# Staging buffers, cast placement and running ahead in the ramp of a fused RWKV-6 and GELU-MLP kernel

## The chip, the cores and the metric

The kernel runs on one core of one Trainium2 chip. The metric is the device time in microseconds (us), and it is taken over several executions. The kernel before takes 254.79 us (median of 3 runs, 253.57 to 255.71). A trace shows one of the executions.

The engines are named as in the profile: PE is the matmul engine (PEld is its weight load), DVE the vector engine, ACT the scalar engine, POOL the general engine, SP the engine whose queue issues the DMAs. "PEclk" or "granted clock" is the share of full speed that PE's clock was granted.

## The reference

A linear-attention recurrence over 768 steps for 4 sequences and 8 heads of width 48 gives a 3072 x 384 matrix. A two-layer MLP with a tanh-GELU follows.

```python
# r, k, v, w: (4, 8, 768, 48) float32; u: (8, 48)
for t in range(S):
    cur = np.einsum('bhd,bhe->bhde', u[None] * kt, vt)
    y[:, :, t] = np.einsum('bhd,bhde->bhe', rt, state + cur)
    state = wt[:, :, :, None] * state + np.einsum('bhd,bhe->bhde', kt, vt)
x = y.transpose(0, 2, 1, 3).reshape(B * S, H * D)        # 3072 x 384
h = x @ w_in                                            # 384 x 2048
g = 0.5 * h * (1.0 + np.tanh(c * (h + 0.044715 * h**3)))
out = g @ w_out                                         # 2048 x 384
```

## The kernel before

The work is cut into 12 units: 3 windows of 256 steps, times 4 sequences. They are numbered from 0. Each unit has these steps.

- `ln`: the log of the decay on ACT. `a1`: cumulative sums of it as matmuls ("cum" in the trace). `exps`: five exponentials on ACT.
- `prep`: on DVE k and r times decay (`kk`, `rq`) and a reduction `dg`; on POOL the cast of v (`vb`), two products for the diagonal (`rk`), the diagonal times v (`vsc`) and the decay masks `am`.
- `attention`, a generator of seven pieces: transposes of rq and kk on PE and their copies on DVE (tiles `T` and `TT`, a2), score matmuls and masks (`mt`, a3, twice), outputs and state (`y`, `p`, a4), two carry-over pieces with ACT copies (`xs`, a5), and the transpose of the result with a DVE copy (`xT`, a6).
- `mm1`: eight pieces of six matmuls each (`h`), each followed by a GELU on ACT (`g`). `mm2`: 32 matmuls (`o`) into two outputs, then `store`.

The kernel loads one function table on ACT for GELU and another for exp and ln, two in each unit. The 25 loads in the trace take 1283 ns each on average, and around one of them ACT goes from the end of a GELU to the start of an exponential in 1.31 us (100.19 to 101.50 us). In a steady unit q, mm1 and mm2 of unit q are threaded with the attention of unit q+1 and the preparation of unit q+2.

Weights arrive as float32 in staging tiles and are cast to bf16:

```python
pload = ctx.enter_context(tc.tile_pool(name="pload", bufs=5))
pstage = ctx.enter_context(tc.tile_pool(name="pstage", bufs=4))
# ...
def load_w_in(i):
    cb, hf = i % NCB, i // NCB
    t = pstage.tile([P, DF // 2], FP, tag="st", name=f"wi{i}")
    SP.dma_start(out=t, in_=moe_w_in[ts(cb, P), ts(hf, DF // 2)])
    stages["i", i] = t
def cast_w_in(i):
    cb, hf = i % NCB, i // NCB
    DVE.tensor_copy(out=w_in_sb[:, cb, ts(hf, DF // 2)], in_=stages.pop(("i", i)))
# load_w_out and cast_w_out alike: tag "st", cast on DVE
```

The start and the loop:

```python
table("exp"); ln(0); a1(0); exps(0)              # joined onto one line here
for i in range(6):
    load_w_in(i)
for nm in ("k", "r", "v"):
    load(1, nm)
ln(1)
prep(0)
load(2, "w")
for _ in attention(0):
    pass
for i in range(6):
    cast_w_in(i)
a1(1); exps(1); ln(2); prep(1)                   # joined here
for i in range(8):
    load_w_out(i)
for nm in ("k", "r", "v"):
    load(2, nm)
load(3, "w")
for q in range(NU):
    # ... loads of unit q+3 and w of unit q+4
    att = attention(q + 1) if q + 1 < NU else iter(())
    table("gelu")
    for i in range(8):
        mm1(q, i)
        if q == 0 and i >= 2:
            cast_w_out(i - 2)
        if i >= 2:
            mm2(q, 0, (2 * i - 4, 2 * i - 3))
        next(att, None)
        if i == 6 and q + 2 < NU:
            a1(q + 2)
    # q == 0: cast_w_out(6), cast_w_out(7)
    table("exp")
    # exps(q + 2), ln(q + 3)
    mm2(q, 0, range(12, 16))
    store(q, 0)
    # prep(q + 2)
    mm2(q, 1, range(16))
    store(q, 1)
    for _ in att:
        pass
```

Four staging tiles serve 14 loads, each load waits for a cast, and every cast stands in DVE's instruction order behind whatever comes before it there.

Of the kernel before, what the change touches and what calls it, by code (L numbers as in the profile page):

```python
# [9 lines left out]
FP = mybir.dt.float32  # L10
BF = mybir.dt.bfloat16
AF = mybir.ActivationFunctionType
AL = mybir.AluOpType
# [6 lines left out]
def kernel(  # L20
# [12 lines left out]
    PE, ACT, DVE, POOL, SP = nc.tensor, nc.scalar, nc.vector, nc.gpsimd, nc.sync  # L33

    B, H, S, D = r.shape
    P = 128
# [8 lines left out]
    NU = len(units)  # L45

    pconst = ctx.enter_context(tc.tile_pool(name="pconst", bufs=1))
    pload = ctx.enter_context(tc.tile_pool(name="pload", bufs=5))
    pstage = ctx.enter_context(tc.tile_pool(name="pstage", bufs=4))
    pfix = ctx.enter_context(tc.tile_pool(name="pfix", bufs=1))  # L50
    pw2 = ctx.enter_context(tc.tile_pool(name="pw2", bufs=2))
    pw3 = ctx.enter_context(tc.tile_pool(name="pw3", bufs=3))
# [10 lines left out]
    def load(q, nm):  # L63
        wi, b = units[q]
        src = {"r": r, "k": k, "v": v, "w": w}[nm]
        t = pload.tile([P, H, 2 * D], FP, tag=nm, name=f"{nm}{q}")
        ap = bass.AP(tensor=src.tensor, offset=src[b, 0, wi * WIN, 0].offset,
                     ap=[[2 * D, P], [S * D, H], [1, 2 * D]])
        SP.dma_start(out=t, in_=ap)
        ld[nm, q] = t  # L70
# [4 lines left out]

    def load_w_in(i):
        cb, hf = i % NCB, i // NCB
        t = pstage.tile([P, DF // 2], FP, tag="st", name=f"wi{i}")
        SP.dma_start(out=t, in_=moe_w_in[ts(cb, P), ts(hf, DF // 2)])
        stages["i", i] = t  # L80

    def cast_w_in(i):
        cb, hf = i % NCB, i // NCB
        DVE.tensor_copy(out=w_in_sb[:, cb, ts(hf, DF // 2)], in_=stages.pop(("i", i)))

    def load_w_out(i):
        t = pstage.tile([P, 2, HD], FP, tag="st", name=f"wo{i}")
        SP.dma_start(out=t, in_=moe_w_out[ds(i * 2 * P, 2 * P), :].rearrange(
            "(ft p) c -> p ft c", p=P))
        stages["o", i] = t  # L90

    def cast_w_out(i):
        DVE.tensor_copy(out=w_out_sb[:, ds(2 * i, 2), :], in_=stages.pop(("o", i)))  # L93

    for nm in ("w", "k", "r", "v"):
        load(0, nm)
# [51 lines left out]
    def table(which):  # L148
        if which == "exp":
            ACT.preload_act_table_set(EXP_SET)  # L150
        else:
            ACT.preload_act_table(AF.Gelu_apprx_tanh)  # L152

    def ln(q):
        lw = logws[q % 3]
        ACT.activation(  # L156
            out=lw[:, :, :, 0:D].rearrange("p t h d -> p h t d"),
            in_=ld.pop(("w", q)).rearrange("p h (t d) -> p h t d", t=2), func=AF.Ln)
# [26 lines left out]
    def prep(q):  # L185
        fq, e1, al = st.pop(("dec", q))
        kt, rt, vt = ld.pop(("k", q)), ld.pop(("r", q)), ld.pop(("v", q))
        kk, rq = kk_ps[q % 2], rq_ps[q % 2]

        def tdh(ap):  # L190
            return ap.rearrange("p h (t d) -> p t h d", t=2)

        def dec(ap):
            return ap.rearrange("p t (h d) -> p t h d", h=H)

        DVE.tensor_tensor(out=kk[:, :, :, 0:D], in0=tdh(kt), in1=dec(e1), op=AL.mult)
        DVE.tensor_tensor(out=rq[:, :, :, 0:D], in0=tdh(rt), in1=dec(fq), op=AL.mult)  # L197
        vb = pw2.tile([P, 2, H, D], BF, tag="vb", name=f"vb{q}")
        POOL.tensor_copy(out=vb, in_=tdh(vt))  # L199
        rk = pw2.tile([P, H, 2, D], FP, tag="rk", name=f"rk{q}", bufs=1)  # L200
        dg = pw2.tile([P, H, 2], FP, tag="dg", name=f"dg{q}")
        vsc = pw2.tile([P, 2, H, D], BF, tag="vsc", name=f"vsc{q}")
        am = pw2.tile([P, 2, G, 2 * D], FP, tag="am", name=f"am{q}")
        POOL.tensor_tensor(out=rk, in0=kt.rearrange("p h (t d) -> p h t d", t=2),  # L204
                           in1=rt.rearrange("p h (t d) -> p h t d", t=2), op=AL.mult)
        POOL.tensor_tensor(out=rk, in0=rk,  # L206
                           in1=u_bc[:, :, None, :].broadcast_to([P, H, 2, D]), op=AL.mult)
        DVE.tensor_reduce(out=dg, in_=rk, axis=AX.X, op=AL.add)  # L208
        POOL.tensor_tensor(  # L209
            out=vsc, in0=vb,  # L210
            in1=dg.rearrange("p h t -> p t h")[:, :, :, None].broadcast_to([P, 2, H, D]),
            op=AL.mult)
        for c2 in range(2):
            POOL.tensor_tensor(
                out=am[:, c2], in0=blk.rearrange("p g j d -> p g (j d)"),
                in1=al[:, :, c2][:, :, None].broadcast_to([P, G, 2 * D]), op=AL.mult)
        st["pre", q] = (kk, rq, vb, vsc, am)

    def a2(q, which):
        kk, rq, vb, vsc, am = st["pre", q]  # L220
# [117 lines left out]
    def mm2(q, c2, fts):  # L338
        g = st["g", q]
        for ft in fts:  # L340
            if ft == 0:
                st["o", q, c2] = ps_o.tile([P, HD], FP, tag="o", name=f"o{q}_{c2}")
            PE.matmul(st["o", q, c2], g[:, ft, ts(c2, P)], w_out_sb[:, ft, :],  # L343
                      start=(ft == 0), stop=(ft == NFT - 1))
# [15 lines left out]
    def attention(q):  # L360
        a2(q, 1)
        a2(q, 0)
        yield
        a3(q, 0)
        yield
        a3(q, 1)
        yield
        a4(q)
        a4p(q)
        yield  # L370
        a5(q, 0)
        yield
        a5(q, 1)
        yield
        a6(q)
        yield

    table("exp")
    ln(0)
    a1(0)  # L380
    exps(0)
    for i in range(6):
        load_w_in(i)
    for nm in ("k", "r", "v"):
        load(1, nm)
    ln(1)
    prep(0)
    load(2, "w")
    for _ in attention(0):
        pass  # L390
    for i in range(6):
        cast_w_in(i)
    a1(1)
    exps(1)
    ln(2)
    prep(1)
    for i in range(8):
        load_w_out(i)
    for nm in ("k", "r", "v"):
        load(2, nm)  # L400
    load(3, "w")
    for q in range(NU):
        if q + 3 < NU:
            for nm in ("k", "r", "v"):
                load(q + 3, nm)
        if q + 4 < NU:
            load(q + 4, "w")
        att = attention(q + 1) if q + 1 < NU else iter(())
        table("gelu")
        for i in range(8):  # L410
            mm1(q, i)
            if q == 0 and i >= 2:
                cast_w_out(i - 2)
            if i >= 2:
                mm2(q, 0, (2 * i - 4, 2 * i - 3))
            next(att, None)
            if i == 6 and q + 2 < NU:
                a1(q + 2)
        if q == 0:
            cast_w_out(6)  # L420
            cast_w_out(7)
        table("exp")
        if q + 2 < NU:
            exps(q + 2)
        if q + 3 < NU:
            ln(q + 3)
        mm2(q, 0, range(12, 16))
        store(q, 0)
        if q + 2 < NU:
            prep(q + 2)  # L430
        mm2(q, 1, range(16))
        store(q, 1)
        for _ in att:
            pass


# [28 lines left out]
```

## Time and profile before

| | before |
|---|---|
| median of 3 runs | 254.79 us |
| span of the profiled run | 253.7 us |
| unit 1's first mm1 on PE | 62.14 us |
| unit 2's first and third mm1 on PE | 86.32 and 90.30 us |
| distance between table loads, steady units | 17.06 us |

The page of the kernel before shows the span in 40 equal slices, each digit being a busy share in tenths. One slice is 6.3 us.

```profile
span 253.7 us, 5753 instructions
...
PE   1527333889289989899899898998998989989993
...
PEclk9999998589959999999999999999999999999999
DMA  8940893339984183291391742913916210020202
```

Read by columns, the first 12 slices (up to 76 us) form a ramp with holes in PE's row. After it PE is at 8 or 9. The DMA row falls to 0 in slice 4 and to 3 in slices 7 to 9, so loads stop in the middle of a phase that still waits for data. The clock falls to 5 in slices 8 and 12. The 9s of the clock row before that don't prove a full clock: this trace's first clock record is at 38.88 us, and the first mm1 piece of unit 0, at 25.77 us, took 1.52 us, where the same six matmuls take 0.82 us later.

The timeline of the DMA queue tells why the loads stop. The columns are start, duration, engine, line, operation and tiles.

```profile
8.79 0.43 SPq L79 DMA_DIRECT2D wi_188<-in_moe_w_in_dram  x1
25.02 0.33 SPq L79 DMA_DIRECT2D wi_190<-in_moe_w_in_dram  x1
...
35.25 0.42 SPq L88 DMA_DIRECT2D wo_411<-in_moe_w_out_dram  x1
45.16 0.37 SPq L88 DMA_DIRECT2D wo_413<-in_moe_w_out_dram  x1
48.37 0.37 SPq L88 DMA_DIRECT2D wo_415<-in_moe_w_out_dram  x1
53.71 0.37 SPq L88 DMA_DIRECT2D wo_417<-in_moe_w_out_dram  x1
...
55.77 3.32 SPq L69 DMA_DIRECT2D v_425<-in_v_dram  x1
```

After four tiles of w_in the queue stands from 9.2 to 25.02 us, until the first cast has freed a tile. It stands again three times between 35.7 and 53.7 us, and v of unit 2 (`v_425`) is behind it.

The waits of PE from 0 to 90 us give the price. The columns are the waiting tile and line, the releaser, the total, the number and the longest.

```profile
PE T_1_447 L225 <- DVE rq_128 L197: 8.3, 1, 8.3
PE mt_0_0_783 L238 <- DVE TT_0_773 L227: 5.7, 1, 5.7
...
PE mt_0_0_1081 L238 <- DVE TT_0_1071 L227: 0.8, 1, 0.8
```

The 8.3 us are unit 1's transposes, which wait for rq and so for unit 1's late r. The 5.7 us are unit 2's scores, which wait for copies that stand in DVE's order behind the reduction `dg`; that waits for POOL's products, which stand behind the cast of unit 2's v on POOL. The 0.8 us return in each steady unit.

PE's timeline shows what follows such a hole; an mm1 piece is six matmuls.

```profile
62.14 0.82 PE L334 MATMUL h_0_745<-xT_651,w_in_sb 128*128 128x256 bf16 x6
...
71.24 1.46 PE L334 MATMUL h_2_804<-xT_651,w_in_sb 128*128 128x256 bf16 x6
...
86.32 0.82 PE L334 MATMUL h_0_1043<-xT_952,w_in_sb 128*128 128x256 bf16 x6
```

A piece takes 0.82 us, but 1.46 us after the 5.7 us hole. The stretch view gives PE's busy time in one steady unit (columns: stretch, its length, then the busy time of each engine, the granted clock, the DMA share, GB/s).

```profile
100.20:117.26 17.06, 15.93 (x209) 11.30 (x208) 11.07 (x16) 10.58 (x19) 7.42 (x6) 1.00 0.52 117
```

So 1.1 us of each steady unit are PE waits.

### The profile page before, as it was taken

The numbers are of one execution on the slowest core, as the hardware profiler recorded it, in microseconds if no ns is written. First come the engines' busy times: TensorE is split into PE (matmuls) and PEld (weight loads), VectorE is DVE, ScalarE is ACT, GpSimd is POOL, SyncE is SP. The second block draws the span as 40 slices with busy tenths as digits, with TensorE's granted clock in tenths as the row PEclk, the third lists the DMA queues.
The fourth block names the chain that finished last, engine by engine and source line by source line (L and its number), as shares of the span: only waits on it lengthen the run. The fifth ranks groups of instructions, "written<-read, shape, count | busy, mean of one in ns | idle before, by whom it ended". The sixth has DMA issues, their size and how long they took to land.

```text
span 253.7 us, 5753 instructions
## 1 busy us (share of the span) xinstructions
PE 204.3 (81%) x2448; PEld 142.2 (56%) x2448; DVE 136.4 (54%) x220; ACT 128.8 (51%) x217; POOL 91.7 (36%) x84
## 2 busy tenths in 40 slices
PE   1527333889289989899899898998998989989993
PEld 0314132455148667576576675766766757657671
DVE  7566335356253663773855757738447377284101
ACT  3401213145514936756649368466584594654760
POOL 2570038000890091470740913806509228040000
PEclk9999998589959999999999999999999999999999
DMA  8940893339984183291391742913916210020202
GB/s 184 317 170 3 249 286 127 106 129 267 267 208 83 32 190 94 62 248 32 95 193 31 181 102 51 242 37 85 215 31 161 60 44 21 6 58 3 48 16 62
DMA packets 56969, 30.45 MB, mean 120 GB/s; under 512 B 50928, under 2 KB 56176, under 8 KB 56944
## 3 DMA queue, kind: packets, MB, share of 16 engines
q1 hardware_dynamic: 56944, 30.09, 48.3%
q8 instruction: 19, 0.31, 0.5%
q14 instruction: 6, 0.05, 0.1%
HBM read 25.36 MB, written 4.72 MB: 119 GB/s over the span
## 4 chain that ended last, share of the span: by engine, by line
PE 46%; DVE 17%; issue 15%; ACT 9%; POOL 7%; DMA 3%; SPq 1%; POOLq 0%; DVEq 0%; ACTq 0%
ACT L150 5%; DMA v_425<-in_v_dram 3%; DVE rq_128 L197 2%; DVE rq_127 L197 1%; PE o_0_3678 L343 1%; PE o_0_3478 L343 1%; PE o_1_3740 L343 1%; PE o_1_3632 L343 1%; POOL rk_205 L204 1%; PE o_0_812 L343 1%; DVE w_out_sb L93 1%; POOL rk_705 L204 1%; POOL rk_705 L206 1%; POOL rk_395 L206 1%; POOL rk_205 L206 1%
## 5 line engine op out<-in xcount | busy, mean ns | idle before, releaser
L334 PEld LDWEIGHTS <-w_in_sb 128*128 128x128 bf16 x576 | 52.8, 101 | 12.1 <-issue 0.9
L150 ACT ACT_TABLE_LOAD x13 | 16.7, 1283 | 0.9 <-PEq L449 0.7
L152 ACT ACT_TABLE_LOAD x12 | 15.4, 1283 | 0.2
L225 PEld LDWEIGHTS <-rq_128 128*128 128x128 bf16 x48 | 3.0, 105 | 11.6 <-DVE rq_128 L197 11.6
L225 PE MATMUL T_1_447<-ident,rq_128 128*128 128x128 bf16 x8 | 1.0, 311 | 8.3 <-DVE rq_128 L197 8.3
L199 POOL CAST vb_703<-v_425 128x768 bf16<-128x768 f32 x1 | 0.8, 825 | 18.9 <-DMA v_425<-in_v_dram 18.9
L199 POOL CAST vb_393<-v_198 128x768 bf16<-128x768 f32 x1 | 0.8, 824 | 17.5 <-DMA v_198<-in_v_dram 17.5
L225 PEld LDWEIGHTS <-rq_127 128*128 128x128 bf16 x48 | 3.0, 105 | 6.0 <-DVE rq_127 L197 6.0
L343 PE MATMUL o_0_507<-w_out_sb,g_438 128*128 128x384 bf16 x16 | 4.4, 370 | 2.0 <-DVE w_out_sb L93 2.0
L156 ACT ACTIVATE logw_124<-w_215 128x768 bf16<-128x768 f32 x1 | 0.8, 846 | 10.1 <-DMA w_215<-in_w_dram 10.1
L343 PEld LDWEIGHTS <-g_438 128*128 128x128 bf16 x32 | 3.2, 103 | 4.7 <-issue 2.8
L209 POOL TENSOR_TENSOR vsc_1005<-vb_1001,dg_1004 128x768 bf16<-128x768 bf16 x1 | 1.5, 1488 | 11.8 <-DVE dg_1004 L208 11.8
L310 ACT ACTIVATE xs_343<-y_0_281 128x384 bf16<-128x384 f32 x1 | 0.5, 493 | 9.5 <-PE y_0_281 L266 9.5
L165 PEld LDWEIGHTS <-strict 128*128 128x128 bf16 x24 | 2.5, 105 | 4.8 <-issue 4.2
L238 PE MATMUL mt_0_0_783<-TT_1_762,TT_0_773 48*64 48x128 bf16 x8 | 0.6, 311 | 5.7 <-DVE TT_0_773 L227 5.7
L209 POOL TENSOR_TENSOR vsc_3381<-vb_3377,dg_3380 128x768 bf16<-128x768 bf16 x1 | 1.5, 1491 | 9.6 <-DVE dg_3380 L208 9.6
L209 POOL TENSOR_TENSOR vsc_1607<-vb_1603,dg_1606 128x768 bf16<-128x768 bf16 x1 | 1.5, 1491 | 9.6 <-DVE dg_1606 L208 9.6
L209 POOL TENSOR_TENSOR vsc_2519<-vb_2515,dg_2518 128x768 bf16<-128x768 bf16 x1 | 1.5, 1490 | 9.6 <-DVE dg_2518 L208 9.6
L209 POOL TENSOR_TENSOR vsc_2810<-vb_2806,dg_2809 128x768 bf16<-128x768 bf16 x1 | 1.5, 1491 | 9.6 <-DVE dg_2809 L208 9.6
L209 POOL TENSOR_TENSOR vsc_2215<-vb_2211,dg_2214 128x768 bf16<-128x768 bf16 x1 | 1.5, 1488 | 9.6 <-DVE dg_2214 L208 9.6
L209 POOL TENSOR_TENSOR vsc_1911<-vb_1907,dg_1910 128x768 bf16<-128x768 bf16 x1 | 1.5, 1487 | 9.6 <-DVE dg_1910 L208 9.6
L209 POOL TENSOR_TENSOR vsc_3099<-vb_3095,dg_3098 128x768 bf16<-128x768 bf16 x1 | 1.5, 1487 | 9.6 <-DVE dg_3098 L208 9.6
(942 smaller groups left out, 697.1 us busy)
## 6 DMA issues: line engine op xcount, KB each, us to landing
wi_182<-in_moe_w_in_dram SPq DMA_DIRECT2D x1, 512.0 KB, 4.9
wi_184<-in_moe_w_in_dram SPq DMA_DIRECT2D x1, 512.0 KB, 5.9
wi_186<-in_moe_w_in_dram SPq DMA_DIRECT2D x1, 512.0 KB, 6.6
wi_188<-in_moe_w_in_dram SPq DMA_DIRECT2D x1, 512.0 KB, 7.4
wi_190<-in_moe_w_in_dram SPq DMA_DIRECT2D x1, 512.0 KB, 4.3
wi_192<-in_moe_w_in_dram SPq DMA_DIRECT2D x1, 512.0 KB, 5.9
w_89<-in_w_dram SPq DMA_DIRECT2D x1, 384.0 KB, 3.8
k_91<-in_k_dram SPq DMA_DIRECT2D x1, 384.0 KB, 4.8
```

What stands on the lines that cost most here:

```text
L93: DVE.tensor_copy(out=w_out_sb[:, ds(2 * i, 2), :], in_=stages.pop(("o", i)))
L150: ACT.preload_act_table_set(EXP_SET)
L152: ACT.preload_act_table(AF.Gelu_apprx_tanh)
L165: PE.matmul(dst[:, 0:HD], s1, lw[:, 1, :, 0:D], start=False, stop=True)
L197: DVE.tensor_tensor(out=rq[:, :, :, 0:D], in0=tdh(rt), in1=dec(fq), op=AL.mult)
L199: POOL.tensor_copy(out=vb, in_=tdh(vt))
L204: POOL.tensor_tensor(out=rk, in0=kt.rearrange("p h (t d) -> p h t d", t=2), in1=rt.rearrange("p h (t d) -> p h t d", t=2), op=AL.mult)
L206: POOL.tensor_tensor(out=rk, in0=rk, in1=u_bc[:, :, None, :].broadcast_to([P, H, 2, D]), op=AL.mult)
L209: POOL.tensor_tensor(out=vsc, in0=vb, in1=dg.rearrange("p h t -> p t h")[:, :, :, None].broadcast_to([P, 2, H, D]), op=AL.mult)
L225: PE.transpose(ps[:, g, :, t2, :], src[:, t2, ds(2 * g, 2), :], ident)
L334: PE.matmul(h[:, f, :], w_in_sb[:, cb, ts(ft, P)], xT[:, cb, :], start=(f + cb == 0), stop=(cb == NCB - 1), skip_group_check=True)
L343: PE.matmul(st["o", q, c2], g[:, ft, ts(c2, P)], w_out_sb[:, ft, :], start=(ft == 0), stop=(ft == NFT - 1))
```

## The change

The intent is to let no early load wait for a cast, to spread the 14 casts over ACT, DVE and POOL, and to let PE run all of mm1 of units 0 and 1 before the attention and mm2 of those units. The core of the diff, with cuts:

```diff
-    pload = ctx.enter_context(tc.tile_pool(name="pload", bufs=5))
-    pstage = ctx.enter_context(tc.tile_pool(name="pstage", bufs=4))
+    pload = ctx.enter_context(tc.tile_pool(name="pload", bufs=4))
+    pstage = ctx.enter_context(tc.tile_pool(name="pstage", bufs=1))
     def load_w_in(i):
-        t = pstage.tile([P, DF // 2], FP, tag="st", name=f"wi{i}")
+        t = pstage.tile([P, DF // 2], FP, tag=f"wi{i}", name=f"wi{i}")
     def load_w_out(i):
-        t = pstage.tile([P, 2, HD], FP, tag="st", name=f"wo{i}")
+        t = pstage.tile([P, 2, HD], FP, tag=f"wi{i}", name=f"wo{i}")
+    def cast(eng, out, in_):        # ACT: activation Copy; others: tensor_copy
# ... prep is split: prep_b(q) holds the reduction dg and vsc, after am
+    for i in range(6):
+        load_w_in(i)
+    # then k, r, v of unit 1; w_out 0-4; w of unit 2; w_out 5-7;
+    # w of unit 3; k, r, v of unit 2: all before the first compute step
# ... attention(0) with prep_b(0) before its fourth piece;
#     casts of w_in: 0, 1, 3 ACT; 2, 5 DVE; 4 POOL
     for q in range(NU):
+        ramp = q < 2
+        if ramp:
+            for i in range(8):
+                mm1(q, i)
+            if q == 0:
+                for i in range(8):
+                    cast_w_out(i, DVE if i in (0, 3, 6) else (ACT if i in (1, 4, 7) else POOL))
         for i in range(8):
-            mm1(q, i)
+            if not ramp:
+                mm1(q, i)
             if i >= 2:
                 mm2(q, 0, (2 * i - 4, 2 * i - 3))
-            next(att, None)
-            if i == 6 and q + 2 < NU:
+            if i in (1, 3, 4, 5, 6, 7):
+                next(att, None)
+            if i == 6 and 0 < q and q + 2 < NU:
                 a1(q + 2)
+        table("exp")
+        if q == 0:
+            ln(2)
+            a1(2)
# ... exps(q + 2), ln(q + 3)
         mm2(q, 0, range(12, 16))
+        if not ramp:
+            for _ in att:
+                pass
         store(q, 0)
# ... prep(q + 2), prep_b(q + 2)
-        mm2(q, 1, range(16))
-        store(q, 1)
+        mm2(q, 1, range(8))
         for _ in att:
             pass
+        mm2(q, 1, range(8, 16))
+        store(q, 1)
```

Two things are not in the intent. The staging tiles are not all apart: w_out 0 to 5 use the tiles of w_in 0 to 5. And the steady units change too: the attention pieces come one mm1 later, and the attention ends before `store(q, 0)` and the preparation of unit q+2.

More of the change, by code (lines that the diff above doesn't have):

```diff
@@ L77, in load_w_in, with cast_w_in @@
         cb, hf = i % NCB, i // NCB
-        t = pstage.tile([P, DF // 2], FP, tag="st", name=f"wi{i}")
+        t = pstage.tile([P, DF // 2], FP, tag=f"wi{i}", name=f"wi{i}")
         SP.dma_start(out=t, in_=moe_w_in[ts(cb, P), ts(hf, DF // 2)])
         stages["i", i] = t
-    def cast_w_in(i):
+    def cast(eng, out, in_):
+        if eng is ACT:
+            ACT.activation(out=out, in_=in_, func=AF.Copy)
+        else:
+            eng.tensor_copy(out=out, in_=in_)
+    def cast_w_in(i, eng):
         cb, hf = i % NCB, i // NCB
-        DVE.tensor_copy(out=w_in_sb[:, cb, ts(hf, DF // 2)], in_=stages.pop(("i", i)))
+        cast(eng, w_in_sb[:, cb, ts(hf, DF // 2)], stages.pop(("i", i)))
     def load_w_out(i):
-        t = pstage.tile([P, 2, HD], FP, tag="st", name=f"wo{i}")
+        t = pstage.tile([P, 2, HD], FP, tag=f"wi{i}", name=f"wo{i}")
         SP.dma_start(out=t, in_=moe_w_out[ds(i * 2 * P, 2 * P), :].rearrange(
@@ L90, in load_w_out, with cast_w_out @@
         stages["o", i] = t
-    def cast_w_out(i):
-        DVE.tensor_copy(out=w_out_sb[:, ds(2 * i, 2), :], in_=stages.pop(("o", i)))
+    def cast_w_out(i, eng):
+        cast(eng, w_out_sb[:, ds(2 * i, 2), :], stages.pop(("o", i)))
     for nm in ("w", "k", "r", "v"):
@@ L207, in prep, with prep_b @@
                            in1=u_bc[:, :, None, :].broadcast_to([P, H, 2, D]), op=AL.mult)
+        for c2 in range(2):
+            POOL.tensor_tensor(
+                out=am[:, c2], in0=blk.rearrange("p g j d -> p g (j d)"),
+                in1=al[:, :, c2][:, :, None].broadcast_to([P, G, 2 * D]), op=AL.mult)
+        st["pre", q] = (kk, rq, vb, vsc, am)
+        st["diag", q] = (rk, dg)
+    def prep_b(q):
+        kk, rq, vb, vsc, am = st["pre", q]
+        rk, dg = st.pop(("diag", q))
         DVE.tensor_reduce(out=dg, in_=rk, axis=AX.X, op=AL.add)
@@ L212, in prep @@
             op=AL.mult)
-        for c2 in range(2):
-            POOL.tensor_tensor(
-                out=am[:, c2], in0=blk.rearrange("p g j d -> p g (j d)"),
-                in1=al[:, :, c2][:, :, None].broadcast_to([P, G, 2 * D]), op=AL.mult)
-        st["pre", q] = (kk, rq, vb, vsc, am)
     def a2(q, which):
@@ L376, in attention @@
         yield
+    for i in range(6):
+        load_w_in(i)
+    for nm in ("k", "r", "v"):
+        load(1, nm)
+    for i in range(5):
+        load_w_out(i)
+    load(2, "w")
+    for i in range(5, 8):
+        load_w_out(i)
+    load(3, "w")
+    for nm in ("k", "r", "v"):
+        load(2, nm)
     table("exp")
@@ L381 @@
     exps(0)
-    for i in range(6):
-        load_w_in(i)
-    for nm in ("k", "r", "v"):
-        load(1, nm)
+    prep(0)
     ln(1)
-    prep(0)
-    load(2, "w")
-    for _ in attention(0):
-        pass
-    for i in range(6):
-        cast_w_in(i)
+    att = attention(0)
+    next(att)
+    next(att)
+    next(att)
+    prep_b(0)
+    next(att)
+    cast_w_in(0, ACT)
+    cast_w_in(1, ACT)
+    cast_w_in(2, DVE)
+    next(att)
+    next(att)
+    next(att)
+    cast_w_in(3, ACT)
+    cast_w_in(4, POOL)
+    cast_w_in(5, DVE)
     a1(1)
     exps(1)
-    ln(2)
     prep(1)
-    for i in range(8):
-        load_w_out(i)
-    for nm in ("k", "r", "v"):
-        load(2, nm)
-    load(3, "w")
+    prep_b(1)
     for q in range(NU):
@@ L409 @@
         table("gelu")
+        ramp = q < 2
[5 more added lines that the diff above has]
+                    cast_w_out(i, DVE if i in (0, 3, 6) else (ACT if i in (1, 4, 7) else POOL))
         for i in range(8):
-            mm1(q, i)
-            if q == 0 and i >= 2:
-                cast_w_out(i - 2)
+            if not ramp:
+                mm1(q, i)
             if i >= 2:
                 mm2(q, 0, (2 * i - 4, 2 * i - 3))
-            next(att, None)
-            if i == 6 and q + 2 < NU:
+            if i in (1, 3, 4, 5, 6, 7):
+                next(att, None)
+            if i == 6 and 0 < q and q + 2 < NU:
                 a1(q + 2)
+        table("exp")
         if q == 0:
-            cast_w_out(6)
-            cast_w_out(7)
-        table("exp")
+            ln(2)
+            a1(2)
         if q + 2 < NU:
@@ L430 @@
             prep(q + 2)
-        mm2(q, 1, range(16))
-        store(q, 1)
+            prep_b(q + 2)
+        mm2(q, 1, range(8))
         for _ in att:
             pass
+        mm2(q, 1, range(8, 16))
+        store(q, 1)
 _INS = ['r', 'k', 'v', 'w', 'u', 'moe_w_in', 'moe_w_out']
```

## The prediction

> **What bounds it now.** The timeline divides the 253.7 us into a ramp, where unit 2's first mm1 starts only at 86.3 us (unit 1's at 62.1), then a steady beat of 17.06 us per unit (table-load starts 100.20, 117.26, 134.32 in the chain), and an end of some 27 us. By stretches, PE is busy 15.9 of 17.05 us in a steady unit, but 5.4 of 18.5, 7.6 of 17.5 and 22.7 of 32 in the first three. The ramp is latency, steady is nearly PE.
>
> Ramp waits read from the timeline:
> - The DMA queue stands from 9.2 to 25.0 us: w_in tile 4 needs a staging buffer whose cast sits behind all of attention 0 on DVE. So the last w_in tile lands at 31.5, k, r, v of unit 1 land at 33.1 to 36, and PE idles 8.3 us before rq.
> - It stands again from 35.7 to 53.7, but for two loads (casts threaded between mask multiplies), so v of unit 2 lands at 63.4, and PE waits 5.7 us at 70.7.
> - mm1 pieces take 1.46 to 1.52 us there, not 0.82; the granted clock was 0.84 and 0.81 in these stretches. [...]
>
> **What the change does.** No work is removed; 14 casts are shared among ACT, POOL and DVE. The queue gets all early loads at once. Not quite "no load waits": w_out 0 to 5 reuse w_in's buffers, but those casts come at about 13 to 24 us, hardly later than the queue needs. At about 1.3 us per 512 KB and 1.1 to 1.5 us per 384 KB (landing spacing), v of unit 1 lands at 23, the last w_out at 34, v of unit 2 at 40.
>
> Estimated walk: attention 0 ends about 1 us earlier (the diagonal reduction now follows the masks); unit 0's mm1 runs 25 to 33, limited by gelu at about 0.75 us each; attention 1 is then exposed, its DVE latency only thinly covered by mm2; a 2.7 us hole for the exp table and ln before the cumulative matmuls; unit 1 starts at about 48, unit 2 at about 68. Its third mm1 comes at 70.6 instead of 90.2: **19.6 us saved**.
>
> **Steady.** Attention's steps move later: transposes after two mm1, so the 0.3 us rq wait and 0.8 us transposed-copy wait should go. In return, xs of half 1 now precedes the exp table on ACT (+0.5 us), and the cumulative matmuls come right behind the state products, so they should wait about 0.5 us for PSUM that DVE's chain (three operations at about 0.66) frees. I estimate 16.6 us per unit: eight times 0.45, **3.6 us saved**.
>
> **Prediction:** 254.8 − 19.6 − 3.6 = 231.6, so about 232 us, range 226 to 240. Chances: faster 0.97, same 0.02, slower 0.01.
>
> **What would show it:** unit 1's and 2's first mm1 at 48 and 68; no queue stand of 10 us; mm1 of unit 0 mostly at 0.82; table-load spacing 16.6; a new PE wait at the cumulative matmuls.
>
> **What would make it wrong:** PE stays at the low clock in unit 0 (+4 us); DMA slower under load, so w_out 6, first in DVE's line before attention 1's copies, lands late; unit 1's xT copy stuck behind unit 3's preparation on DVE; steady waits larger (+3.6) or smaller (−3).

In the walk, 0.75 us per GELU and 2.7 us for the exp table and ln are estimates; the trace of the kernel before shows 0.60 us for a GELU (39.50 us), 1.28 us for a table load (38.20 us) and 0.85 us for an ln (37.34 us).

## More of the kernel before

One more line matters later: beside no POOL work, a w_out cast costs DVE 0.55 us (DVE's timeline).

```profile
44.58 0.55 DVE L93 CAST w_out_sb<-wo_405 128x768 bf16<-128x768 f32 x1
```

## The result, and the profile after

| | before | after |
|---|---|---|
| median of 4 runs, same chip | 254.53 us | 236.18 us (235.43 to 237.72) |
| ratio | | 0.9285, 95% interval 0.9223 to 0.9346 |
| span of the profiled run | 253.7 us | 235.9 us |
| unit 1's first mm1 | 62.14 us | 53.74 us |
| unit 2's first and third mm1 | 86.32, 90.30 us | 74.04, 77.89 us |
| distance of table loads, steady | 17.06 us | 16.56 us |

A ratio is the mean time of one kernel's runs over that of the other's in the same rounds, so it is not quite the ratio of the medians. Executions over 1.5% slower than the fastest of the same kernel are left out of the means. The outputs are correct. The profiled run is the slowest of the four (237.72 us), so single moments in it can lie a microsecond late. Two of the kernels below, e1_steady_undone and e4_a1_late, have the same ramp up to unit 2's start, and their traces show by how much: unit 1 starts at 52.71 and 52.69 us there, unit 2 at 73.01 and 72.98 us. In e1_steady_undone:

```profile
52.71 5.97 PE L345 MATMUL h<-xT,w_in_sb 128*128 128x256 bf16 x48 [0.46 <-DVE xT L331]
```

So a start of unit 1 that is a microsecond ahead of 53.74 us shows nothing yet, and what the experiments below gain against 53.74 us is about 1 us less against these two.

The difference of the spans is 17.8 us. Up to unit 2's third mm1 the kernel gains 90.30 - 77.89 = 12.4 us; the other 5.4 us come in the steady part after it. (In e4_a1_late that third mm1 comes at 75.97 us, a gain of 14.3 us; its profile is the fastest of its four runs.) The page, in slices of 5.9 us:

```profile
span 235.9 us, 5759 instructions
...
PE   0456787598895999999999999999999999999992
...
PEclk9999996779997999999999999999999999999998
DMA  7999999713902911942923914915719120020202
```

The DMA row now stays at 9 through slices 2 to 7. PE's row has no slice under 5 from slice 3 to the last but one, yet its clock falls to 6 and 7 in slices 7 to 9 and again in slice 13. The DMA queue:

```profile
8.69 0.44 SPq L79 DMA_DIRECT2D wi_161<-in_moe_w_in_dram  x1
9.16 0.47 SPq L79 DMA_DIRECT2D wi_163<-in_moe_w_in_dram  x1
...
23.15 0.37 SPq L94 DMA_DIRECT2D wo_177<-in_moe_w_out_dram  x1
...
34.41 1.38 SPq L69 DMA_DIRECT2D v_197<-in_v_dram  x1
```

The fifth w_in tile is issued at 9.16 us instead of 25.02, and v of unit 2 at 34.41 instead of 55.77. The queue stands only about 1.4 us before `wo_177`, which reuses the tile of w_in 2. PE's waits from 0 to 90 us:

```profile
PE cum_0_658 L170 <- ACT logw_124 L162: 2.7, 1, 2.7
PE h_0_1043 L345 <- DVE xT_1020 L331: 2.4, 1, 2.4
PE mt_0_0_537 L249 <- DVE TT_0_530 L238: 2.1, 1, 2.1
...
PE h_0_745 L345 <- DVE xT_722 L331: 1.1, 1, 1.1
```

The waits of 8.3 and 5.7 us are gone, and four new ones stand here. PE's timeline places them:

```profile
37.26 0.82 PE L354 MATMUL o_0_532<-w_out_sb,g_437 128*128 128x384 bf16 x2
...
46.18 0.32 PE L170 MATMUL cum_0_658<-logw_124,strict 128*128 128x384 bf16 x1 [2.73 <-ACT logw_124 L162]
...
53.74 0.82 PE L345 MATMUL h_0_745<-xT_722,w_in_sb 128*128 128x256 bf16 x6 [1.06 <-DVE xT_722 L331]
...
74.04 1.31 PE L345 MATMUL h_0_1043<-xT_1020,w_in_sb 128*128 128x256 bf16 x6 [2.37 <-DVE xT_1020 L331]
75.14 1.49 PE L345 MATMUL h_1_1051<-xT_1020,w_in_sb 128*128 128x256 bf16 x6
```

Two mm2 matmuls take 0.49 us at the full clock (at 33.45 us in the same trace) and 0.82 us at 37.26 us. Unit 2 waits for its xT for 2.37 us and then runs two mm1 pieces at 1.31 and 1.49 us instead of 0.82. DVE's timeline and, under it, POOL's show why the copies `TT` came late:

```profile
31.49 1.09 DVE L86 CAST w_out_sb<-wo_173 128x768 bf16<-128x768 f32 x1
32.50 1.84 DVE L86 CAST w_out_sb<-wo_179 128x768 bf16<-128x768 f32 x1
34.26 1.17 DVE L86 CAST w_out_sb<-wo_187 128x768 bf16<-128x768 f32 x1
35.36 0.68 DVE L238 COPY TT_1_519<-T_1_510 128x1024 bf16<-128x1024 bf16 x1
```

```profile
30.55 1.62 POOL L215 TENSOR_TENSOR am_421<-blk,al_408 128x384 f32<-128x384 bf16 x2
32.12 1.81 POOL L225 TENSOR_TENSOR vsc_420<-vb_416,dg_419 128x768 bf16<-128x768 bf16 x1
33.87 1.15 POOL L86 CAST w_out_sb<-wo_177 128x768 bf16<-128x768 f32 x1
```

The same cast that took DVE 0.55 us takes 1.09, 1.84 and 1.17 us here. Each of the three ends 0.41 us after a POOL instruction ends: 32.58 after 32.17, 34.34 after 33.93, and 35.43 after 35.02 (start plus duration on either side). So these three casts look as if they waited for POOL's instructions to end; the trace shows the times, not the cause. Not every DVE instruction does: the first copy `TT` took 0.68 us at 35.36 us and ended at 36.04, while POOL's next cast ran from 34.97 to 36.12 us.

One steady unit of the kernel after, in the stretch view:

```profile
104.94:121.50 16.56, 15.89 (x209) 11.42 (x208) 10.18 (x16) 10.51 (x18) 8.22 (x6) 1.00 0.54 121
```

The waits for rq (0.3 us) and for the copies (0.8 us) are gone; PE now waits 0.4 us for a GELU and 0.3 us at the second cumulative matmul, for ACT's copy `xs`.

### The profile page after: what moved, and what is told of

The parts are those of the page before. It is cut to its first block, busy times and chain, and to the rows that moved or that the text cites. A ratio compares the mean times of both kernels' runs of the same rounds, so it can differ in the third digit from the quotient of the medians.

```text
span 235.9 us, 5759 instructions
## 1 busy us (share of the span) xinstructions
PE 203.4 (86%) x2448; PEld 143.0 (61%) x2448; DVE 131.3 (56%) x211; ACT 134.0 (57%) x223; POOL 104.5 (44%) x87
## 4 chain that ended last, share of the span: by engine, by line
PE 54%; ACT 19%; DVE 11%; issue 9%; POOL 3%; DMA 2%; DVEq 0%; ACTq 0%; POOLq 0%
ACT L156 5%; DVE w_out_sb L86 2%; DMA w_89<-in_w_dram 2%; PE o_0_532 L354 1%; DVE rq_127 L203 1%; ACT logw_124 L162 1%; PE o_0_3678 L354 1%; PE o_0_3457 L354 1%; PE o_0_3175 L354 1%; PE o_1_3740 L354 1%; PE o_1_3632 L354 1%; PE o_1_3389 L354 1%; POOL rk_418 L210 1%; POOL rk_418 L212 1%; ACT logw_122 L162 1%
## 5 line engine op out<-in xcount | busy, mean ns | idle before, releaser
L345 PEld LDWEIGHTS <-w_in_sb 128*128 128x128 bf16 x576 | 54.0, 99 | 21.1 <-issue 9.9
L215 POOL TENSOR_TENSOR am_997<-blk,al_975 128x384 f32<-128x384 bf16 x2 | 2.4, 1230 | 12.5 <-ACT al_975 L187 12.5
L215 POOL TENSOR_TENSOR am_1304<-blk,al_1273 128x384 f32<-128x384 bf16 x2 | 2.4, 1229 | 11.5 <-ACT al_1273 L187 11.5
L215 POOL TENSOR_TENSOR am_1608<-blk,al_1577 128x384 f32<-128x384 bf16 x2 | 2.4, 1230 | 8.3 <-ACT al_1577 L187 8.3
L215 POOL TENSOR_TENSOR am_1912<-blk,al_1881 128x384 f32<-128x384 bf16 x2 | 2.4, 1230 | 8.3 <-ACT al_1881 L187 8.3
L215 POOL TENSOR_TENSOR am_2216<-blk,al_2185 128x384 f32<-128x384 bf16 x2 | 2.4, 1230 | 8.3 <-ACT al_2185 L187 8.3
L215 POOL TENSOR_TENSOR am_2520<-blk,al_2489 128x384 f32<-128x384 bf16 x2 | 2.4, 1228 | 8.3 <-ACT al_2489 L187 8.3
L215 POOL TENSOR_TENSOR am_2811<-blk,al_2780 128x384 f32<-128x384 bf16 x2 | 2.4, 1228 | 7.9 <-ACT al_2780 L187 7.9
L215 POOL TENSOR_TENSOR am_3100<-blk,al_3069 128x384 f32<-128x384 bf16 x2 | 2.4, 1228 | 7.9 <-ACT al_3069 L187 7.9
L215 POOL TENSOR_TENSOR am_3382<-blk,al_3352 128x384 f32<-128x384 bf16 x2 | 2.4, 1228 | 7.9 <-ACT al_3352 L187 7.9
L354 PE MATMUL o_0_532<-w_out_sb,g_437 128*128 128x384 bf16 x16 | 5.5, 469 | 0.2 <-ACT w_out_sb L84 0.2
L236 PEld LDWEIGHTS <-rq_127 128*128 128x128 bf16 x48 | 3.4, 104 | 3.3 <-DVE rq_127 L203 3.2
L354 PEld LDWEIGHTS <-g_437 128*128 128x128 bf16 x32 | 3.3, 117 | 3.2 <-issue 2.5
L170 PE MATMUL cum_0_201<-logw_122,strict 128*128 128x384 bf16 x1 | 0.5, 479 | 5.4 <-ACT logw_122 L162 5.4
L362 DVE COPY ob_3736<-o_0_3678 128x384 f32<-128x384 f32 x1 | 0.6, 558 | 7.7 <-PE o_0_3678 L354 7.7
L215 POOL TENSOR_TENSOR am_699<-blk,al_677 128x384 f32<-128x384 bf16 x2 | 2.3, 1187 | 4.3 <-ACT al_677 L187 4.3
L354 PEld LDWEIGHTS <-g_3653 128*128 128x128 bf16 x32 | 3.0, 98 | 1.7 <-ACT g_3653 L347 0.4
L238 DVE COPY TT_1_818<-T_1_809 128x1024 bf16<-128x1024 bf16 x1 | 0.7, 692 | 6.0 <-PE T_1_809 L236 6.0
L354 PE MATMUL o_0_3678<-w_out_sb,g_3653 128*128 128x384 bf16 x16 | 3.8, 327 | 0.0
```

What stands on the lines that cost most here:

```text
L215: POOL.tensor_tensor(out=am[:, c2], in0=blk.rearrange("p g j d -> p g (j d)"), in1=al[:, :, c2][:, :, None].broadcast_to([P, G, 2 * D]), o ...
L236: PE.transpose(ps[:, g, :, t2, :], src[:, t2, ds(2 * g, 2), :], ident)
L345: PE.matmul(h[:, f, :], w_in_sb[:, cb, ts(ft, P)], xT[:, cb, :], start=(f + cb == 0), stop=(cb == NCB - 1), skip_group_check=True)
L354: PE.matmul(st["o", q, c2], g[:, ft, ts(c2, P)], w_out_sb[:, ft, :], start=(ft == 0), stop=(ft == NFT - 1))
```

## The experiments

The questions: are the parts of the gain independent of each other, and why did the ramp gain 12.4 us and not the predicted 19.6? Theory A held that the shortfall arises while attention of unit 1 stands exposed, from 33 to 54 us, through three things: DVE casts stretched by POOL ahead of the copies, PE at half clock, and DVE's order that puts preparation ahead of xT; and that running mm1 ahead is itself what exposes the attention and costs time. Its rivals are stated at each run. All ten kernels gave correct results. In three calls to the chip, each call's kernels shared a chip and the runs of the kernel before (medians 255.00, 254.29 and 254.41 us). All times are device times unless a line says otherwise; moments come from one profile each.

| run | median us (range) | ratio to before | 95% interval |
|---|---|---|---|
| the change | 236.18 (235.43 to 237.72) | 0.9285 | 0.9223 to 0.9346 |
| e1_steady_undone | 241.94 (241.00 to 243.15) | 0.9503 | 0.9451 to 0.9554 |
| e6_not_ahead | 242.54 (240.54 to 245.36) | 0.9498 | 0.9437 to 0.9558 |
| e7_loads_only | 248.05 (247.78 to 248.21) | 0.9737 | 0.9689 to 0.9784 |
| e4_a1_late | 230.60 (229.76 to 231.07) | 0.9051 | 0.9008 to 0.9094 |
| e2_copies_first | 235.07 (233.59 to 236.17) | 0.9241 | 0.9191 to 0.9292 |
| e8_casts_on_act | 233.46 (233.02 to 233.71) | 0.9180 | 0.9165 to 0.9194 |
| e3_fill | 234.53 (233.10 to 235.93) | 0.9216 | 0.9200 to 0.9233 |
| e5_xt_first | 232.06 (231.55 to 232.62) | 0.9127 | 0.9107 to 0.9147 |
| b1_three | 223.31 (221.23 to 224.10) | 0.8763 | 0.8709 to 0.8817 |
| b2_ln_early | 218.57 (218.43 to 218.66) | 0.8589 | 0.8558 to 0.8620 |

The run of 245.36 us of e6_not_ahead was slow and is not in its ratio, but it is in its median and range; the median of the three fast runs is 242.47 us.

### e1_steady_undone: the steady order of before

```diff
-            if i in (1, 3, 4, 5, 6, 7):
+            if not ramp or i in (1, 3, 4, 5, 6, 7):
                 next(att, None)
@@
-        if not ramp:
-            for _ in att:
-                pass
         store(q, 0)
```

> The changed kernel with attention's steps from unit 2 on put back to where they stood before (one step after every mm1 piece, the last transposes drained at the end). Theory A, my sum: the changed kernel's 18.3 us gain is two independent parts, a ramp of about 12.3 us (third mm1 of unit 2 at 78.1 instead of 90.4) and a steady part of about 5.6 us (from there to the third mm1 of unit 10: 130.6 instead of 136.2). Then this kernel takes 236.2 + 5.6 = about 242 us, its table-load spacing returns to 17.06, and unit 2's third mm1 stays within 2 us of 78. Rival B: the shorter beat comes from the ramp having loaded further ahead, not from the new places of the steps; then it takes about 236 and the spacing stays near 16.6.

Measured: 241.94 us, 5.8 us more than the change. The table loads are 17.03 us apart again, and PE waits 0.8 us for the copies and 0.3 us for rq in each unit, as before. Unit 1 started at 52.71 and unit 2 at 73.01 us. So the steady gain comes from the new order of the attention (its pieces later, its end earlier), and it adds to the ramp's gain. This run undoes both parts of that order at once and doesn't tell them apart.

### e6_not_ahead: everything but mm1 running ahead

```diff
-        if ramp:
-            for i in range(8):
-                mm1(q, i)
-            # ... and the eight casts of w_out here
         for i in range(8):
-            if not ramp:
-                mm1(q, i)
+            mm1(q, i)
+            if q == 0 and i >= 2:
+                cast_w_out(i - 2, DVE if i in (2, 5) else (ACT if i in (3, 6) else POOL))
@@
         if q == 0:
+            cast_w_out(6, DVE)
+            cast_w_out(7, ACT)
             ln(2)
```

> The changed kernel, but mm1 of units 0 and 1 is not run ahead: mm1 pieces alternate with mm2 and attention steps as in the other units, and the w_out casts follow the pieces, on the same three engines. Theory A: running mm1 ahead costs more than it gives, because it leaves attention 1 and 2 exposed with only mm2 to cover their DVE latency (PE idle and at half clock from 34 to 54 us in the changed kernel). Then this kernel is faster: unit 1's first mm1 at 46 to 50 instead of 53.7 and 229 to 234 us in all. Rival B, the intent of the change: running ahead fills PE while attention waits, and without it the ramp is 3 to 8 us longer, 239 to 244 us.

Measured: 242.47 us in the fast runs. Unit 1 starts at 60.71, unit 2 at 78.80 us, and its third piece comes at 82.65 instead of 77.89. PE's waits from 30 to 84 us in this kernel:

```profile
PE T L236 <- DVE rq L203: 4.3, 1, 4.3
PE cum L170 <- ACT logw L162: 3.5, 1, 3.5
PE o L354 <- ACT w_out_sb L84: 2.8, 2, 1.4
```

With the pieces threaded, the first transposes stand in PE's order behind two mm1 pieces, and mm1 stops there for rq. Run ahead, the whole of mm1 fills that wait. The w_out casts move too in this run, to places between the pieces, and the 2.8 us on ACT's casts, with 2.3 us on DVE's, are waits for them (0.2 us in the change). So this part of Theory A fell: running ahead, with the casts behind it, is worth about 6 us (6.3 by the medians of fast runs, 5.4 by the ratios), and does not cost any. How much of that is the place of the casts was not tested. (The stretch from 34 to 54 us in the change, which the expectation calls half clock, had a mean granted clock of 0.74, with 0.50 from 36.66 to 43.49 and from 46.91 to 50.32 us.)

### e7_loads_only: the kernel before with the new loads and staging

```diff
 # against the kernel before
-    pload ... bufs=5        pstage ... bufs=4
+    pload ... bufs=4        pstage ... bufs=1
-        t = pstage.tile([P, DF // 2], FP, tag="st", name=f"wi{i}")
+        t = pstage.tile([P, DF // 2], FP, tag=f"wi{i}", name=f"wi{i}")
 # ... w_out alike; all early loads issued first, in the order of the change;
 # casts stay on DVE and in their places
```

> The kernel before with only the loads changed: every weight tile of w_in has its own staging buffer (w_out 0 to 5 take them over, as in the changed kernel), pload 4, and all early loads issued at the start in the changed kernel's order. Casts, their engine (DVE) and the order of the steps stay as before. Theory A: the ramp's 12.3 us are mainly the loads; then unit 2's third mm1 comes at 76 to 80 instead of 90.4 and the time is 254.5 - 12 = about 241 to 245 us with a spacing of 17.06. Rival B: the loads alone give little, because casts on DVE and the order then bind: 249 us or more.

Measured: 248.05 us, between what the two theories gave. Unit 1 starts at 62.19 us, just as before (62.14). Unit 2 starts at 79.05 us, its third piece at 83.03. So the 7 us come wholly after unit 1's first mm1, where the 5.7 us wait and the half clock around its end (0.50 from 69.60 to 76.43 us in the kernel before) were. Before unit 1, the earlier data gain nothing. The six w_in casts, all on DVE and beside POOL's preparation of unit 1, took 7.36 us together, and alone they take 0.69 us each.

Loads (248.05), then casts on three engines, the early attention order and the steady order (242.47), then running ahead (236.18): this chain of kernels splits the gain into 7.0, 5.6 and 6.3 us. In the ramp, the middle step moved unit 2's third piece by only 0.4 us (83.03 to 82.65); the rest of its 5.6 us is about the steady part that e1_steady_undone measured.

### e4_a1_late: the cumulative matmuls after the last attention piece, in steady units

```diff
+            if not ramp and i == 7:
+                next(att, None)
+                if q + 2 < NU:
+                    a1(q + 2)
             if i >= 2:
                 mm2(q, 0, (2 * i - 4, 2 * i - 3))
-            if i in (1, 3, 4, 5, 6, 7):
+            if i in (1, 3, 4, 5, 6) or (ramp and i == 7):
                 next(att, None)
-            if i == 6 and 0 < q and q + 2 < NU:
+            if i == 6 and q == 1:
                 a1(q + 2)
```

> The changed kernel, but from unit 2 on the cumulative matmuls of the unit after next stand behind the last mm1 piece and the last state product instead of two pieces earlier, so the last gelu, the xs copy and the exp table load start earlier and run under them. Theory A: a steady unit is a loop of PE (third mm1 to last mm1) and ACT (last gelu, xs copy, exp table, five exps, ln, gelu table, first gelu); the cumulative matmuls are in PE's half and cost 1.2 us plus a 0.3 us wait for the xs copy to free PSUM. Then the table-load spacing falls from 16.56 to about 15.6 and the time by 6 to 8 us to about 229. Rival B: PE's own work bounds a unit at 16 us or more; then the spacing falls by less than 0.5 and the time by under 3 us.

Measured: 230.60 us, 5.6 us less than the change and a little under the 6 to 8 us expected. Table loads are 15.49 us apart. The stretch view of one steady unit:

```profile
101.36:116.85 15.49, 15.49 (x211) 11.49 (x210) 10.72 (x16) 10.54 (x19) 8.48 (x6) 1.00 0.58 130
```

PE is busy for all 15.49 us. What the prediction feared at the cumulative matmuls was real, and moving them by one step removes it, the wait for the GELU too. PE's busy time itself fell from 15.89 to 15.49 us for the same matmuls; the ends of matmuls are modelled in this profile, and I did not settle what those 0.4 us are.

### e2_copies_first: two of DVE's three w_out casts after the copies

```diff
                 for i in range(8):
-                    cast_w_out(i, DVE if i in (0, 3, 6) else (ACT if i in (1, 4, 7) else POOL))
+                    if i not in (3, 6):
+                        cast_w_out(i, DVE if i == 0 else (ACT if i in (1, 4, 7) else POOL))
@@
                 next(att, None)
+            if q == 0 and i == 1:
+                cast_w_out(3, DVE)
+                cast_w_out(6, DVE)
```

> The changed kernel, but two of DVE's three w_out casts (tiles 3 and 6) are issued behind the copies of attention 1's transposes instead of ahead of them. In the changed kernel those two took 1.84 and 1.17 us and the copies began at 35.36, although the transposes were done at 33.6. Theory A: the copies wait for the casts; then they begin at about 33.3, unit 1's first mm1 comes 1.5 to 3 us earlier than 53.74, and the time falls by 1.5 to 3 us. Rival B: the cost is only moved, because tile 3 is then cast late for mm2; then unit 1's first mm1 stays within 0.7 us of 53.7.

Measured: 235.07 us. In the profile the copies start at 33.03 us instead of 35.36, the mm2 pairs take 0.49 us, and unit 1 starts at 51.28. But of the four runs two took 233.6 and 234.0 us at granted clocks of 0.991 and 0.985, and two took 236.2 us at 0.975 and 0.970. The profile is one of the former. By its interval this run cannot be told from the change, and the expected 1.5 to 3 us are not shown: the mechanism is seen in the profile, and the gain came in only half of the runs.

### e8_casts_on_act: DVE's three w_out casts on ACT

```diff
-                    cast_w_out(i, DVE if i in (0, 3, 6) else (ACT if i in (1, 4, 7) else POOL))
+                    cast_w_out(i, POOL if i in (2, 5) else ACT)
```

> The changed kernel with DVE's three w_out casts moved to ACT (six on ACT, two on POOL). Theory A: what mattered is DVE's line ahead of the copies and that DVE's and POOL's instructions stretch each other (DVE casts of 0.55 us alone took 1.09, 1.84 and 1.17 us beside POOL); then the copies begin at about 33.2, POOL's vsc and casts shorten to about 1.5 and 1.0 us or less, and unit 1 begins 1.5 to 3 us earlier than 53.74. Rival B: ACT, which starts its casts only after the last gelu at 33.2 and needs 0.73 us each, becomes the new line for mm2: tile 0 at 34, the last tile at 37.7, and unit 1 begins within 0.7 us of 53.7.

Measured: 233.46 us, with all four runs within 0.7 us and an interval clear of the change's. The stretch from 34 to 54 us, first of the kernel after, then of this one (PE, PEld, DVE, ACT, POOL, clock):

```profile
34.00:54.00 20.00, 13.90 (x141) 7.58 (x141) 13.40 (x17) 8.48 (x14) 9.55 (x8) 0.74 0.67 150
```

```profile
34.00:54.00 20.00, 14.47 (x164) 8.68 (x164) 9.94 (x14) 12.24 (x20) 11.12 (x10) 0.91 0.70 154
```

DVE's timeline of this kernel:

```profile
33.15 1.29 DVE L238 COPY TT<-T 128x1024 bf16<-128x1024 bf16 x2 [1.88 <-PE T L236]
```

DVE now waits for PE and not the reverse. The two POOL casts took 1.59 us together, now with no DVE casts around them, instead of 1.15 us each. The clock in the stretch rose from 0.74 to 0.91. Unit 1 starts at 51.22. The earlier copies and the higher clock come together here, so this run does not tell their shares. Sharing the casts over all three engines was worse here than leaving DVE out.

### e3_fill: PE kept busy with matmuls that nobody reads

```diff
+    def fill(n):
+        d = ps_h.tile([P, 2, WIN], FP, tag="h", name="fill")
+        for j in range(n):
+            PE.matmul(d[:, 0, :], w_in_sb[:, 0, 0:P], w_in_sb[:, 1, 0:WIN],
+                      start=(j == 0), stop=(j == n - 1), skip_group_check=True)
@@
+            if q == 0 and i == 3:
+                fill(18)
@@
             ln(2)
+            fill(24)
             a1(2)
```

> The changed kernel with 42 filler matmuls in unit 0 (18 before attention 1's third step, 24 before unit 2's cumulative matmuls), in holes where PE waits anyway; their result is never read, and the outputs stay right. Theory A: PE's half clock from 37 to 50 us is itself a cost; with the holes filled the clock stays up, mm2 pairs take 0.49 instead of 0.82 us, and unit 1's first mm1 comes 1.5 to 3 us earlier than 53.74. Rival B: in that stretch PE waits for DVE and ACT at almost every step, so a faster PE waits longer; unit 1 begins within 0.7 us of 53.7.

Measured: 234.53 us in 6 runs. The stretch from 34 to 54 us:

```profile
34.00:54.00 20.00, 17.58 (x216) 12.40 (x215) 11.69 (x17) 10.90 (x18) 11.96 (x10) 1.00 0.75 162
```

The clock is 1.00 throughout, and unit 1 starts at 51.96 us although 42 useless matmuls were added and the first filler delayed a step. That is 1.8 us sooner than in the profile of the change, but only 0.7 us sooner than in the two other traces of that ramp, which is Rival B's bound. What decides is the stretch from the first copy `TT` to unit 1's first mm1, which leaves out that mm1 of unit 0 ended 1.35 us later here (its granted clock from 24.70 to 37 us was 0.86, and 0.99 in the change): 16.73 us, against 18.38 us in the change and 17.74 us in each of e1_steady_undone and e4_a1_late, all three with low clock in it (twelve mm2 matmuls took 4.00 us in e1_steady_undone and 3.98 in e4_a1_late, and 2.11 here; the change's clock is given under e6_not_ahead). So the half clock is a cost of its own, apart from the waits, of 1.0 to 1.7 us in that stretch. The total is weaker evidence: this interval and that of the change overlap by a little (0.9223 to 0.9233). Later, unit 2 (at 72.26 us) still met a low clock after a gap that nothing filled: its first twelve mm1 matmuls took 2.46 us instead of 1.47.

That idle PE is what lowers the clock fits this run, 1.00 against 0.74 in the stretch with the holes filled. No least length of a gap is shown. In the kernel after, the granted clock was 1.00 from 26.43 to 36.66 us and 0.50 from 36.66 to 43.49, and the half-speed matmuls from 36.68 us on came after a single gap of 2.07 us. Again it was 1.00 from 50.32 to 74.21 us and 0.50 from 74.21 to 77.62, and the gap ahead of unit 2's first mm1 at 74.04 was 2.37 us long. But a gap of the same 2.37 us ahead of unit 2 went before a low clock here, and before the full clock in e2_copies_first and e8_casts_on_act: the twelve matmuls after it took 1.47 us in each, and the clock from 54 to 78 us was 1.00. So a gap of this length may or may not be followed by half speed, and what decides it is not shown.

### e5_xt_first: xT ahead of the next preparation on DVE in the ramp too

```diff
-        if not ramp:
-            for _ in att:
-                pass
+        for _ in att:
+            pass
         store(q, 0)
```

> The changed kernel, but units 0 and 1 end as the others do: attention's last transposes and their copy xT stand before the output copy and before the preparation of the unit after next, instead of behind it on DVE. In the changed kernel PE waited 1.06 us at 53.74 and 2.37 us at 74.04 for that copy, and ran the next two mm1 pieces of unit 2 at half clock. Theory A: the order on DVE alone is the cause; then unit 1 begins at about 52.7 to 53.0, unit 2 at about 70.5 to 71.5 with pieces of 0.82 us, and the time falls by 3 to 5 us. Rival B: PE, which then needs xs of half 1 earlier, only waits there instead: under 1 us.

Measured: 232.06 us, 4.1 us less than the change. Unit 1 starts at 51.37 us with no wait for xT; unit 2 starts at 69.23 at full clock, and its third piece comes at 71.95 instead of 77.89.

```profile
69.23 1.47 PE L345 MATMUL h<-xT,w_in_sb 128*128 128x256 bf16 x12
...
71.95 0.82 PE L345 MATMUL h<-xT,w_in_sb 128*128 128x256 bf16 x6 [0.36 <-ACT g L347]
```

Unit 1 starts earlier than the 52.7 to 53.0 expected, but 0.9 us of that were there before the edit acts (unit 2's cumulative matmuls at 45.32 instead of 46.18). Two lines of scheduling return both waits for xT (1.06 and 2.37 us) and the half clock behind the second.

### b1_three: e4_a1_late, e5_xt_first and e8_casts_on_act together

The edit is the three diffs above.

> The changed kernel with three of the edits that helped alone: DVE's w_out casts on ACT, xT before the preparation in units 0 and 1, and the cumulative matmuls behind the last piece from unit 2 on. If the three gains are independent (2.5 us at unit 1's start, partly the same 1 to 2 us as the next one's, about 2.4 and another 2.4 at unit 2's start, and about 6 to 8 us in the steady units): unit 1 begins at about 49.4 and unit 2 at about 67.3, table-load spacing 15.5, time 221 to 224 us. If they lean on the same wait: 226 us or more.

Measured: 223.31 us. Unit 1 starts at 49.30, unit 2 at 68.29 and its third piece at 71.01 us, which are nearly the predicted moments (48, 68 and 70.6); the beat is 15.48 us. One run of the four took 221.23 us, with a mean clock of 1.000; the others had 0.981 to 0.991 and took 222.7 to 224.1 us.

### b2_ln_early: b1_three, with unit 2's log and cumulative sums made earlier

```diff
 # against b1_three
     load(1, "w")
+    load(2, "w")
@@
     ln(1)
+    ln(2)
     att = attention(0)
@@
-        table("exp")
         if q == 0:
-            ln(2)
             a1(2)
+        table("exp")
```

> The same as the run beside it, and unit 2's w is loaded right after unit 1's and its logarithm taken before the first gelu table, so that in unit 0 the cumulative matmuls of unit 2 no longer wait for the exp table and the logarithm (in the changed kernel PE stands 2.73 us there). Theory A: that hole is on the path, all of it; then unit 1 begins 2 to 3 us earlier than in the run beside it, at about 47, and the time falls by 2 to 3 us to about 219 to 221. Rival B: the hole only moves, since the exponentials still wait for the table and the preparation on DVE for them; then less than 1 us. Weights land 1.3 us later, which should not matter, since unit 0's first mm1 needs them at 24.8.

Measured: 218.57 us, with all four runs within 0.3 us: 14% under the kernel before (254.41 us on this chip), and the fastest of all. Unit 1 starts at 45.04, unit 2 at 62.89 us. Its page and its stretch from 34 to 54 us:

```profile
PE 194.7 (90%) x2448; PEld 140.8 (65%) x2448; DVE 129.9 (60%) x208; ACT 136.3 (63%) x226; POOL 106.2 (49%) x87
...
PE   0464977999899999999999999999999999999992
...
PEclk9999999999999999999999999999999999999999
```

```profile
34.00:54.00 20.00, 18.61 (x243) 12.34 (x243) 12.53 (x18) 14.39 (x23) 14.67 (x12) 1.00 0.84 197
```

The gain of 4.7 us is more than the 2.73 us of the hole that was taken out. The rest goes with the clock, which no longer falls: the trace of b1_three has a mean granted clock of 0.91 from 34 to 54 us and of 0.93 from 54 to 78 us, this one has 1.00 in both. The run of b1_three that happened to keep the full clock lies 2.7 us above this kernel's median, which is about the hole alone. That is a single run without a kept trace, so this split is likely, and not shown.

What was not tried: really separate staging for all 14 loads. (No run shows it; a kernel with w_out on tiles of its own was refused by the build.)

## Why the prediction was right or wrong

236.18 us lies in the range 226 to 240, 4 us above the point.

**What held.** The queue's stands of 15.8 us and, in three pieces, some 17 us vanished, and so did the waits of 8.3 and 5.7 us. The hole for the exp table and ln was predicted at 2.7 us and measured at 2.73. The steady beat was predicted at 16.6 us and measured at 16.56. The distance from unit 1's to unit 2's first mm1 was predicted at 20 us (48 to 68) and measured at 20.3; that is partly luck, since 2.37 us of it are the wait for unit 2's xT, which the sum did not hold.

**Which term was mis-sized.** "Its third mm1 comes at 70.6 instead of 90.2: 19.6 us saved." It came at 77.89, so 12.4 us were saved in the profiled run. The 7.3 us that are missing lie in two places: 5.7 us before unit 1's first mm1 ("unit 1 starts at about 48", measured 53.74) and 1.3 us between unit 2's first and third mm1 (2.6 us predicted, 3.85 measured); 0.3 us lie between. Some of this belongs to the profiled run alone: in e1_steady_undone and e4_a1_late unit 1 starts at 52.7 us, and in e4_a1_late the third mm1 comes at 75.97, 5.4 us behind the prediction. The steps that made it so:

- The step "attention 1 is then exposed, its DVE latency only thinly covered" has no figure for the three casts ahead of the copies; the list of risks names w_out 6 "first in DVE's line before attention 1's copies", but fears only that it lands late. Beside POOL the three casts took 4.1 us in all instead of 1.65, and the copies began at 35.36 instead of about 33.1. Moving the casts to ACT (e8_casts_on_act) gave 2.7 us by the medians, a part of it by the clock.
- The prediction expected "mm1 of unit 0 mostly at 0.82", which came, and named the low clock as a risk there. The clock fell later, after the exposed wait, from about 37 us on (0.50 from 36.66 to 43.49 us); e3_fill shows that this is a cost of its own. In e8_casts_on_act and b2_ln_early the clock of the stretch from 34 to 54 us rose (from 0.74 to 0.91 and 1.00) together with other repairs.
- xT behind the preparation on DVE stood in the list of risks, "unit 1's xT copy stuck behind unit 3's preparation". It happened in both ramp units, though with other names: unit 1's behind unit 2's preparation (1.06 us) and unit 2's behind unit 3's (2.37 us, and half clock after it). A risk that can be read from the program order could have been put into the sum. e5_xt_first shows its worth: 4.1 us.

These three overlap, since each later start depends on all the earlier ones and the clock on the gaps (0.74 from 34 to 54 us in the change, 1.00 with two of them filled in e3_fill). So the gains of the single repairs (2.7, 1.6 and 4.1 us by the medians) cannot be read as shares of the 7.3 us; some of the same microseconds are in more than one of them. With two of these repairs and the steady one in place, b1_three has the predicted moments within 1.3 us.

**The steady part** was undersized: 3.6 us predicted, 5.4 in the spans, 5.8 by undoing it. That the total came so near is in part luck: a saving in the ramp that was put 7.2 us too high and one in the steady part 1.8 us too low cancel in part. The beat was right. The sum was eight times 0.45 us. From unit 2's third mm1 to unit 10's the same eight beats took 130.6 us after and 136.3 before, so 0.71 us each: the units of the last window, which keep less state, save more (16.23 us against 17.07) than the middle ones that I took for all.

**The expected wait at the cumulative matmuls** was in the trace, at 0.3 us instead of 0.5. Its releaser by the profile was mostly ACT's copy `xs`, which must free a PSUM tile, and not DVE's state chain. Its worth was larger than that wait: moving the cumulative matmuls gave 5.6 us (e4_a1_late).

**A belief of mine that fell** after the result: that running mm1 ahead cost more than it gave. Without it, and with the casts moved to suit, the kernel is about 6 us slower (e6_not_ahead). And the change's first part, the loads, is worth 7 of the 18 us (e7_loads_only), all of it after unit 1's start.

## What to carry to other kernels

When a stall is taken out of a ramp, cost the chain that is then exposed with durations measured beside the engines that will be running, not with those of an idle neighbour: a DVE cast of 0.55 us became 1.84 us beside POOL. Then look at each engine's program order for small copies that the critical engine needs and that stand behind work for a later unit; putting them first cost nothing and gave 4 us. Last, count gaps of 2 us on PE twice, once as a wait and once as the half-speed matmuls that may follow (2.37 us, then two mm1 pieces of 1.31 and 1.49 us instead of 0.82), because a repair that closes the last gap returns both.
